# The searched run of a deep cross network kernel ends one tile further back, and the last tail phase too

## The chip, the cores and the metric

The kernel runs on one core of one Trainium2 chip. The metric is the device time in microseconds (us) of one execution. A core has a matrix engine (TensorE, PE in the profile), a vector engine (VectorE, DVE), a scalar engine (ScalarE, ACT), GpSimd (POOL) and a queue engine for DMA (SyncE, SP). They run side by side and wait for each other through semaphores. TensorE writes its results into PSUM, which has eight banks of 128 x 512 floats.

## The reference

```python
B, F, D, L = 16384, 26, 16, 6          # Din = F * D = 416
def reference(x0, ws, bs):             # x0 [B, 416], ws [6, 416, 416], bs [6, 416], all bf16
    x = x0
    for l in range(6):
        proj = jnp.einsum('bd,de->be', x, ws[l]) + bs[l]
        x = x0 * proj + x
    return x
```

Six layers follow one another. Each multiplies the running x by a 416 x 416 matrix, adds a bias, multiplies by the first input x0 element by element and adds x.

## The kernel before, in words

**Jobs, tiles, chunks.** The 16384 rows are cut into eight groups g of 2048 rows, and a job (g, l) is layer l of group g. In all but the last job the features lie on the partitions and the rows on the free axis. The 416 features are three blocks of 128 and a rest of 32. So a job has three tiles i = 0, 1, 2 of 128 output features, each cut into four chunks j of 512 rows, and a tail of 32 output features. The running x of a job lies in `xs` (three blocks) and `x3s` (the rest of 32, whose four chunks lie on the four quarters of the partitions).

**Two ways to compute a tile.** In the full way (`full`, line 659, and `rows32`, line 680) a tile is 12 matmuls that use all 128 rows of the array (three blocks by four chunks) and four matmuls 32 rows deep, one on each quarter of the array's rows, which run side by side. Tiles are paired so that the four-row parts of two neighbours stand together: mode "FR" does the full part first, "RF" the rows first, and "F1" is a single one that cuts its row part into pieces (line 674). In the searched run (`stream`, lines 1035 and 1039) every matmul is 32 rows deep. A chunk is then 13 matmuls, three for each of the four row groups and one more for the row group that holds its rest of 32. The four row groups work side by side on different chunks, and each row group adds into the chunk's bank in turn: within one chunk a row group waits until the one before it is through. `weave` searches for an order of these matmuls; four of them, one in each row group, take the place of one full matmul.

**Tails.** The 32 tail features of two or three jobs are computed together in a tail phase (`tails`, lines 694 and 706), one bank for each job, with four groups of 32 columns of the array side by side. A job (g, l + 1) needs the tail of (g, l).

**The order.** `items` is the list of all tiles and tail phases, and `where` says after which tile each tail phase stands. The searched run covers `items[s_lo:s_hi]`. What follows it is done in the full way: before the change these are the tiles (6,4)0, (6,4)1, (6,4)2, (7,4)0, (6,5)0, then the last tail phase with the tails of (7,4) and (6,5), then (6,5)1, (6,5)2, (7,4)1, (7,4)2. The last job, (7,5), comes after these in another form: rows on the partitions, four steps kk of four banks each (`nat_full`, line 1119, with ScalarE's copy on line 1171, VectorE's multiplication on line 1177 and addition on line 1183, and stores on line 1190).

**Evacuation.** ScalarE adds the bias and copies a bank to `tw` (line 574 in the searched run, 539 in the full way, 617 for tails). VectorE multiplies by x0 (lines 583, 548, 619) and adds x (lines 586, 553, 621). In the full way two neighbouring banks are read by one instruction, if their numbers follow one another.

**The output of group 6.** When the tail and the three tiles of (6,5) are done, `output(6)` puts on SP's queue, in this order: the transposing DMAs of feature block 0 and of block 1 from `xs` into `ost` (line 887), that of the tail into `ot3` (line 895), and two of half of block 2 (line 887). All DMAs of this end are issued by SP in program order, and each waits on SP for what it reads. The tail is copied from `ot3` into its place in `ost` by ScalarE (`spread("act")`, line 914). This copy stands in ScalarE's queue behind the evacuation of tile (7,4)1 and ahead of that of (7,4)2. `rest_turn(0)` and `rest_turn(1)` (line 935) transpose the results of (7,4)0 and (7,4)1 for the last job's additions, and two stores of group 6 (line 923) follow on SP's queue behind them.

Of the kernel before, what the change touches and what calls it, by code (L numbers as in the profile page):

```python
# [21 lines left out]
class Program:  # L22
# [12 lines left out]
    def add(self, eng, fn, reads=(), writes=(), lane=None, batch=None, hold=False, release=False, row=None):  # L35
        op = Op(eng, fn, lane, batch, row)
        deps = {}
        if eng == "pool":
            writes = list(writes) + ["pool"]
        for t in reads:  # L40
            w = self.writer.get(t)
            if w is not None:
                deps[id(w)] = (w, True)
        for t in writes:
            w = self.writer.get(t)
            if w is not None:
                deps[id(w)] = (w, True)
            for r in self.readers.get(t, ()):
                if id(r) not in deps:
                    deps[id(r)] = (r, False)  # L50
        for d, raw in deps.values():
            if d.lane is None and d.eng == eng and lane is None and (eng == "pe" or not raw):
                if row is None or d.row is None or row == d.row:
                    continue
            op.deps.append(d)
        for t in reads:
            self.readers.setdefault(t, []).append(op)
        for t in writes:
            self.writer[t] = op
            self.readers[t] = []  # L60
        if eng == "dve":
            if hold:
                self.flush()
                self.held = op
            else:
                self.queue[eng].append(op)
                if release:
                    self.flush()
        else:
            self.queue[eng].append(op)  # L70
        if lane is not None:
            batches = self.lanes.setdefault(lane, [])
            if not batches or batches[-1][0] != batch:
                batches.append((batch, []))
            batches[-1][1].append(op)
        return op
# [254 lines left out]
def bass_standalone__cross_network_dcn__recsys_kernel(  # L331
# [7 lines left out]
    L = ws.shape[0]  # L339
# [6 lines left out]
    LAST = NG - 1  # L346
# [9 lines left out]
    batches = []  # L356
# [582 lines left out]

    items = []  # L940
    where = {(b[0 if b in batches[4:-3] else min(1, len(b) - 1)], 0): b for b in batches[:-1]}
    where[((LAST - 1, L - 1), 0)] = batches[-1]
    del where[((0, 0), 0)]
    where[((0, 1), 0)] = where.pop(((1, 0), 0))
    tiles = [((1, 0), 0), ((1, 0), 1), ((0, 1), 0), ((0, 1), 1), ((0, 1), 2), ((1, 0), 2)]
# [11 lines left out]
    single = 0  # L957
    k = 0
    while k < len(items):
        if items[k][0] == "tails":  # L960
            if single % 2 == 0:
                nxt = k + 1
                if nxt < len(items) and items[nxt][0] == "tile":
                    items[k], items[nxt] = items[nxt], items[k]
                    single += 1
                    k += 1
            single = 0
        else:
            single += 1
        k += 1  # L970

    W_LOAD = {(1, 0): 3, (0, 2): 4, (1, 1): 5}
# [20 lines left out]
    mode = {}  # L993
    prev = None
    for n, it in enumerate(items):
        if it[0] == "tails":
            prev = None
        elif prev is None:
            mode[n] = "FR"
            prev = n  # L1000
        else:
            mode[n] = "RF"
            prev = None
# [61 lines left out]

    first_job()
    add("pool", lambda h: h.memset(brow[:, :], 0.0), writes=["brow"])
    s_lo, s_hi = items.index(("tile", (0, 2), 1)), items.index(("tile", (6, 4), 0))
    for n, it in enumerate(items):
        if n == s_lo:  # L1070
            stream(items[s_lo:s_hi])
# [196 lines left out]
```

## Time and profile before

| what | us |
|---|---|
| median of 3 runs | 472.18 (472.04 to 472.39) |
| the profiled execution: its time | 472.21 |
| the profiled execution: its span, first to last instruction | 470.4 |
| TensorE busy | 462.1 (98% of the span) |
| VectorE busy | 403.4 (86%) |
| ScalarE busy | 379.1 (81%) |
| the searched run ends, the full way begins | 424.18 |
| last tail phase (line 694, then 706) | 438.69 to 440.53 |
| tile (7,4)2 ends on TensorE | 452.18 |
| its last addition ends on VectorE | 456.92 |
| the last store is issued | 467.12 |

All places in the span are counted from its first instruction. A busy time is the sum over the instructions of an engine; instructions on one engine overlap a little, so that two additions of 0.69 us each may be shown as 1.28 us together. The chain that ended last is followed back from the last instruction, at each step to what released it. The profiled execution's 1.81 us outside the span are start and end that the trace does not show.

### The profile page before, as it was taken

How to read it: one execution, taken by the hardware profiler on the slowest of the kernel's cores; microseconds unless marked ns; L12 is line 12 of the kernel's file. 1: busy time of each engine (PE TensorE's matmuls, PEld its weight loads, DVE VectorE, ACT ScalarE, POOL GpSimd, SP SyncE). 2: the span in 40 equal slices, each digit the busy share in tenths (PEclk: the TensorE clock that was granted, in tenths of full speed). 3: DMA queues.
4: the chain of work that ended last, by engine and by line, in shares of the span. 5: the costliest groups of instructions: out<-in, count | busy, mean ns of one | idle time of the engine just before them, and what ended most of it. 6: DMA issues, size and time to landing. Idle time of an engine off the chain costs nothing.

```text
span 470.4 us, 17240 instructions
## 1 busy us (share of the span) xinstructions
PE 462.1 (98%) x7718; PEld 268.0 (57%) x7725; DVE 403.4 (86%) x700; ACT 379.1 (81%) x598; POOL 8.4 (2%) x15
## 2 busy tenths in 40 slices
PE   9999999999999999999999999999999999999995
PEld 5444476665655557566666567565455665653442
DVE  2897988888889888988989898988989888988887
ACT  4687788787878788787988878888788887877775
POOL 1000000000000000010001000000000000000000
PEclk9999999999999999999999999999999999999999
DMA  8985849101002967094667993880000194139689
GB/s 225 185 175 141 159 113 186 30 3 26 2 5 34 184 189 143 19 146 148 134 105 114 227 146 81 169 248 3 25 2 3 29 167 124 34 59 216 127 148 293
DMA packets 139086, 53.75 MB, mean 114 GB/s; under 512 B 112762, under 2 KB 138500, under 8 KB 139012
## 3 DMA queue, kind: packets, MB, share of 16 engines
q1 hardware_dynamic: 138856, 52.54, 53.1%
q8 instruction: 60, 0.98, 0.9%
q10 hardware_dynamic: 156, 0.11, 0.1%
q14 instruction: 14, 0.11, 0.1%
HBM read 5.97 MB, written 13.63 MB: 42 GB/s over the span
## 4 chain that ended last, share of the span: by engine, by line
PE 92%; DVE 5%; ACT 1%; DMA 1%; issue 0%; DVEq 0%; SPq 0%; ACTq 0%
PE ps L1035 67%; PE ps L659 7%; PE ps L1039 6%; PE ps L706 6%; PE ps L647 2%; PE ps L694 1%; DVE x L1183 1%; PE ps L680 1%; DVE x L1177 1%; PE ps L778 1%; ACT tw L539 1%; DVE x L553 1%; DVE tw L548 1%; DMA ot<-x 1%; DVE x L586 1%; DVE tw L583 1%
## 5 line engine op out<-in xcount | busy, mean ns | idle before, releaser
L1035 PE MATMUL ps<-x,wm 32*128 32x512 bf16 x5856 | 349.9, 375 | 0.6 <-DVE ts L613 0.6
L574 ACT ACTIVATE tw<-ps,bias 128x512 bf16<-128x512 f32 x488 | 305.1, 687 | 42.0 <-PE ps L1035 26.9
L1035 PEld LDWEIGHTS ps<-x,wm 32*128 32x128 bf16 x5856 | 213.5, 92 | 123.4 <-issue 3.2
L583 DVE TENSOR_TENSOR tw<-tw,x 128x1024 bf16<-128x1024 bf16 x244 | 166.0, 690 | 41.2 <-ACT tw L574 40.5
L586 DVE TENSOR_TENSOR x<-tw,x 128x1024 bf16<-128x1024 bf16 x244 | 158.3, 686 | 0.4
L1039 PE MATMUL ps<-x,w 32*128 32x512 bf16 x488 | 147.6, 374 | 0.0
L539 ACT ACTIVATE tw<-ps,bias 128x1024 bf16<-128x1024 f32 (+1 forms) x48 | 40.7, 917 | 14.9 <-PE ps L680 11.7
L1039 PEld LDWEIGHTS ps<-x,w 32*128 32x128 bf16 x488 | 42.0, 92 | 5.8
L659 PE MATMUL ps<-x,wm 128*128 128x512 bf16 x181 | 41.3, 380 | 1.0 <-issue 1.0
L617 ACT ACTIVATE ts<-ps,bias 128x512 bf16<-128x512 f32 x33 | 21.0, 685 | 20.4 <-PE ps L694 20.4
L706 PE MATMUL ps<-x,wm 128*32 128x512 bf16 x564 | 33.6, 380 | 0.0
L659 PEld LDWEIGHTS ps<-x,wm 128*128 128x128 bf16 x188 | 17.3, 98 | 23.8 <-issue 3.8
L548 DVE TENSOR_TENSOR tw<-tw,x 128x1024 bf16<-128x1024 bf16 (+1 forms) x41 | 25.5, 634 | 5.2 <-ACT tw L539 4.9
L553 DVE TENSOR_TENSOR x<-tw,x 128x1024 bf16<-128x1024 bf16 (+1 forms) x41 | 24.4, 631 | 0.0
L706 PEld LDWEIGHTS ps<-x,wm 128*32 128x32 bf16 x564 | 13.5, 96 | 17.8 <-ACT tw L574 3.4
L621 DVE TENSOR_TENSOR x<-ts,x 128x512 bf16<-128x512 bf16 x47 | 18.3, 418 | 0.0
L613 DVE SCALAR_TENSOR_TENSOR ts<-ps,bias,x 128x512 bf16<-128x512 f32 x14 | 10.5, 749 | 6.1 <-PE ps L694 5.9
L916 POOL COPY ost<-ot 128x512 bf16<-128x512 bf16 x6 | 7.0, 1158 | 413.4 <-DMA ot<-x 413.4
L619 DVE TENSOR_TENSOR ts<-ts,x 128x512 bf16<-128x512 bf16 x33 | 13.6, 418 | 0.0
L1119 PE MATMUL ps<-wm,x 128*128 128x416 bf16 x48 | 9.8, 340 | 0.7 <-DVE x L553 0.7
L1171 ACT ACTIVATE x<-ps 128x416 bf16<-128x416 f32 x16 | 7.7, 517 | 2.1 <-PE ps L1119 1.9
L806 DVE COPY x<-ps 128x512 bf16<-128x512 bf16 x5 | 2.0, 423 | 8.4 <-PE ps L796 8.3
(50 smaller groups left out, 78.2 us busy)
## 6 DMA issues: line engine op xcount, KB each, us to landing
out_dram<-ost SPq DMA_DIRECT2D x6, 1664.0 KB, 8.2
x<-x SPq DMA_DIRECT2D x24, 96.0 KB, 2.2
x<-in_x_dram SPq DMA_DIRECT2D x8, 208.0 KB, 4.3
x<-in_x_dram SPq DMA_DIRECT2D x4, 416.0 KB, 6.8
out_dram<-ost SPq DMA_DIRECT2D x2, 832.0 KB, 5.6
wm<-in_ws_dram SPq DMA_DIRECT2D x5, 312.0 KB, 3.5
x<-x SPq DMA_DIRECT2D x22, 64.0 KB, 2.2
out_dram<-x SPq DMA_DIRECT2D x3, 416.0 KB, 4.8
```

The lines of the kernel that those rows point to most:

```text
L539: add("act", lambda h, a=a, w=w, b0=b0: h.activation(tw[r][:, a * CH:(a + w) * CH], psum[:, b0 * CH:(b0 + w) * CH], ACT_F.Identity, bias=b ...
L548: add("dve", lambda h, a=a, e=e: h.tensor_tensor(tw[r][:, a * CH:e * CH], tw[r][:, a * CH:e * CH], x0s[s0][:, i * GC + a * CH:i * GC + e * ...
L553: add("dve", lambda h, a=a, e=e: h.tensor_tensor(xs[so][:, i * GC + a * CH:i * GC + e * CH], tw[r][:, a * CH:e * CH], src(i, a, e), ALU.ad ...
L574: add("act", lambda h: h.activation(tw[r][:, j * CH:(j + 1) * CH], bank(b), ACT_F.Identity, bias=bias[:, i, l:l + 1], scale=1.0), reads=[( ...
L583: add("dve", lambda h: h.tensor_tensor(tw[r][:, o], tw[r][:, o], x0s[s0][:, c], ALU.mult), reads=[("tw", r, k) for k in both] + [x0_tok(s0 ...
L586: add("dve", lambda h: h.tensor_tensor(xs[so][:, c], tw[r][:, o], src(i, a, a + 2), ALU.add), reads=[("tw", r, k) for k in both] + [stok(i ...
L617: add("act", lambda h: h.activation(ts[r][:, :], bank(b), ACT_F.Identity, bias=bias[:, 3, l:l + 1], scale=1.0), reads=[("ps", b), "bias"], ...
L621: add("dve", lambda h: h.tensor_tensor(x3s[so][:, :], ts[r][:, :], res, ALU.add), reads=[("ts", r)] + rtok, writes=[("x3", so), ("x3", so, ...
L659: add("pe", lambda h, t=t, j=j, k=k, w=w: h.matmul(bank(banks[j])[:, k * w:(k + 1) * w], wm[l][:, t, ecols], src(t, j, j + 1)[:, k * w:(k ...
L706: add("pe", lambda h, t=t, j=j, src=src, l=l, b=b, ro=ro, qo=qo: h.matmul(psum[qo, b * CH:(b + 1) * CH], wm[l][:, t, NT * P:D], src(t, j, ...
L1035: add("pe", lambda h, l=l, t=t, j=j, b=b, q=q, ecols=ecols, src=src, kw=kw: h.matmul(bank(b), wm[l][q, t, ecols], src(t, j, j + 1)[q, :], ...
L1039: add("pe", lambda h, l=l, b=b, q=q, ecols=ecols, s3=s3, kw=kw: h.matmul(bank(b), w3[l][q, ecols], s3[q, :], **kw), reads=tok3 + [("w3", l ...
```

## The change

The last tail phase is attached to tile (6,5)1 in place of (6,5)0, so that three tiles follow it in place of four. The searched run ends before tile (6,4)1 in place of (6,4)0. The pairing of the tiles, which decides their modes, begins anew at (6,4)1, and so does the count `single` that decides whether a tail phase is moved by one tile.

```diff
     items = []
     where = {(b[0 if b in batches[4:-3] else min(1, len(b) - 1)], 0): b for b in batches[:-1]}
-    where[((LAST - 1, L - 1), 0)] = batches[-1]
+    where[((LAST - 1, L - 1), 1)] = batches[-1]
+    behind = ("tile", (LAST - 1, L - 2), 1)
...
         else:
-            single += 1
+            single = 1 if items[k] == behind else single + 1
         k += 1
...
     for n, it in enumerate(items):
+        if it == behind:
+            prev = None
         if it[0] == "tails":
             prev = None
...
-    s_lo, s_hi = items.index(("tile", (0, 2), 1)), items.index(("tile", (6, 4), 0))
+    s_lo, s_hi = items.index(("tile", (0, 2), 1)), items.index(behind)
```

The end of the list of items, with the modes, before:

```
searched run ... (7,3)1 (7,3)2 |
(6,4)0 FR, (6,4)1 RF, (6,4)2 FR, (7,4)0 RF, (6,5)0 F1, tails (7,4)+(6,5),
(6,5)1 FR, (6,5)2 RF, (7,4)1 FR, (7,4)2 RF
```

and after:

```
searched run ... (7,3)1 (7,3)2 (6,4)0 |
(6,4)1 FR, (6,4)2 RF, (7,4)0 FR, (6,5)0 RF, (6,5)1 F1, tails (7,4)+(6,5),
(6,5)2 FR, (7,4)1 RF, (7,4)2 RF
```

The line numbers of the kernel after are three higher from `stream` on.

## The prediction

> **What bounds the kernel now.** I read first the page's busy times and then the chain that ended last, because the change touches only the end of the order.
>
> ```profile
> PE 462.1 (98%) x7718; PEld 268.0 (57%) x7725; DVE 403.4 (86%) x700; ACT 379.1 (81%) x598; POOL 8.4 (2%) x15
> ```
>
> TensorE is busy in 98% of the span, and nothing in the change takes matmuls away. So any gain has to come from the stretch in which TensorE no longer sets the end. The chain, in order of time, says where that begins:
>
> ```profile
> 440.53 2.59 PE ps L647 x48
> 443.12 0.37 PE ps L680 x4
> 443.48 2.27 ACT tw L539 x3
> ...
> 448.87 0.61 DVE x L553
> 449.49 0.16 SPq L887
> 449.64 0.05 issue
> 449.69 2.96 DMA ot<-x
> 452.65 0.02 issue
> 452.67 0.63 ACT ost L914
> 453.30 1.16 ACT tw L539 x2
> ...
> 456.25 0.67 DVE x L553 x2
> 456.92 1.20 DVE x L1139 x2
> 458.12 0.49 DVE x L1177
> 458.61 0.44 issue
> ```
>
> TensorE leaves the chain at 443.48. From there it runs over the additions of the tiles behind the tail phase, SP, the transposition of group 6's tail (ot<-x) and ScalarE's copy of it (L914), behind which the evacuation of (7,4)2 is queued. From 454 to 466.8 it is VectorE. The timeline shows what VectorE (first four rows) and ScalarE (next four) waited for:
>
> ```profile
> 450.66 0.69 DVE L548 TENSOR_TENSOR tw<-tw,x 128x1024 bf16<-128x1024 bf16 x1 [0.58 <-ACT tw L539]
> 451.66 0.69 DVE L548 TENSOR_TENSOR tw<-tw,x 128x1024 bf16<-128x1024 bf16 x1 [0.32 <-ACT tw L539]
> 453.91 0.42 DVE L548 TENSOR_TENSOR tw<-tw,x 128x512 bf16<-128x512 bf16 x1 [0.35 <-ACT tw L539]
> 454.49 0.43 DVE L548 TENSOR_TENSOR tw<-tw,x 128x512 bf16<-128x512 bf16 x1 [0.15 <-ACT tw L539]
> ...
> 445.96 2.12 ACT L539 ACTIVATE tw<-ps,bias 128x1024 bf16<-128x1024 f32 x2 [0.22 <-PE ps L659]
> 449.36 2.27 ACT L539 ACTIVATE tw<-ps,bias 128x512 bf16<-128x512 f32 x3 [1.28 <-PE ps L680]
> 452.67 0.63 ACT L914 ACTIVATE ost<-ot 128x512 bf16<-128x512 bf16 x1 [1.04 <-DMA ot<-x]
> 453.21 2.40 ACT L539 ACTIVATE tw<-ps,bias 128x512 bf16<-128x512 f32 x4
> ```
>
> VectorE stands idle for 0.58 + 0.32 + 0.35 + 0.15 = 1.40 us between 450.07 and 456.92, and ScalarE for 1.04 us on the tail's transposition. Last I read the DMAs of the last 13.4 us (40 slices from 457.0 to 470.4):
>
> ```profile
> DMA  0999999999999999999999999999999999930000
> ```
>
> The DMA engines are full from 457.4 to 468.7, so the stores could set the end as well.
>
> **The change part by part.** The order of the instructions is the same in both kernels up to the middle of the stretch ahead of the searched run's last tail phase.
>
> *(6,4)0 goes into the searched run.* The full way gives 24 matmuls in 5.13 us, 0.214 us each; a tile is 12 of these and one slot of rows, 13 slots or 2.78 us, and so are four chunks in the searched run (52 matmuls, four to a slot). What follows on TensorE up to the tile in 32-column pieces (L647) is the same sequence of full tiles, rows and tail phase, one tile's name further on, with as many switches between the forms. So that tile ends later by 2.78 us plus what the run's end loses more than before. Before, 90 matmuls follow the run's last tail phase: 22.5 slots, 4.82 us; they take 418.15 to 424.18, 6.03 us, so 1.21 are lost, to row groups that wait for another one in the same bank and to the run-out, where some row groups have finished. After, 138 matmuls follow it, and 4 more stand ahead of it. The new list ends with four matmuls all on row group 3, behind chunks that the other three have finished; the old one ends with two on one row group. Following both lists row group by row group at 0.214 us, with a short pause wherever a chunk passes to another row group, gives 5.84 us for the old one (6.03 measured) and 8.87 for the new one. With one slot for the 4 matmuls ahead that is 3.24 us more, against 2.78: **0.46 us lost**. Bounds: nothing (a run-out as good as before), and 1.21 (the loss of this stretch once more). I take 0.46, as the same counting came within 0.2 us of the measured row.
>
> *Three tiles behind the tail phase.* The piece tile ends at 443.12 + 3.24 = 446.36; it is now (6,5)2. By the distances before, ScalarE begins its evacuation 0.35 us later, at 446.71, and needs 2.12 (two pairs of banks; the instruction list shows whole pairs for all these tiles, against 2.27 with a split pair before): 448.83. VectorE must be free by then: its tail work, which ended at 444.33, moves by 3.24 to 447.57, ahead of the first pair at 447.8. Then a multiplication of 0.69 and two additions, 1.28 together and overlapping by 0.08, end at 450.74. (7,4)1 is "RF" now, so its evacuation waits for no rows behind it: its full part begins 0.70 us behind the piece tile, at 447.06, and ends 2.57 later at 449.63; ScalarE starts 0.42 ahead of that (as at 445.96 before, where the tile in the middle ended at 446.38) and ends at 451.33. VectorE does (7,4)1 in 2.48 us without a wait, up to 453.22.
>
> *The tail's transposition.* On SP, block 1 of group 6 waited for VectorE until 447.66, was issued at 447.69 and held SP for 1.95 us; the tail followed at 449.69. Now block 1 is (6,5)1, ahead of the tail phase, and its last addition moves from (6,5)0's 442.99 by 3.24 to 446.23. SP issues it until 448.2, and the tail, ready at 447.57, is issued then and lands 2.96 later, at 451.2: as ScalarE comes free at 451.33. The wait of 1.04 goes. The copy (0.54 us up to the next start) ends at 451.87, and (7,4)2's four evacuations at 454.3; TensorE has its last chunk by 452.8. VectorE, which comes to them at 453.2, now finds them ready: eight operations at 0.347 (the seven from 454.49 to 456.92) end at 456.0. **0.92 us earlier** than 456.92; the 1.40 us of idle time go, and 0.46 of lost run-out and small shifts come off.
>
> *Behind it.* SP's later issues follow: the halves of block 2 (2.64 us for both) from 450.15, the transpositions of (7,4)1 from 452.8 (454.15 before), the stores of group 6 from 456.0 (457.36), 1.36 earlier. The 0.44 us "issue" at 458.61 stands ahead of the additions that read the transposed (7,4)1; this wait shrinks by up to 0.43, of which at most 0.2 reaches the end, since ScalarE's last copy ends at 465.97 and VectorE takes it up at about 466.2. The last store (104 KB) lands 2.8 us after its issue; small copies on the chip land after 2.2 in the median (64 and 96 KB), so up to 0.6 of it is waiting behind full DMA engines, which start 1.36 earlier. From these the end moves by 0.92 at least and 0.92 + 0.6 at most; I take 1.3, near the DMAs' 1.36, since they are full to the end. All other work moved (evacuation of (6,4)0 by single chunks, 4 x 0.69 on ScalarE in place of 2.12) lies beside TensorE: ScalarE and VectorE both stood idle between 420 and 427 (VectorE for 1.84 us, ScalarE for 1.08), and both wait for TensorE again before the tail phase.
>
> The sum: the profiled execution's 472.21 (span 470.4 and 1.81 around it; 0.03 above the median, so no correction) less 1.3 is **470.9**.
>
> **The rivals.**
>
> *The run's end costs more.* In the new list 13 chunks follow the last tail phase, and ScalarE needs 0.6 to 0.69 us for each plus 1.26 for the tails. The first full tile takes its fourth bank from the last chunk but one, which ScalarE, counted from the chunks' ends at these prices, leaves at 427.9 to 428.2; TensorE wants it at 428.2. With the upper price and the row groups' bound of 1.21, TensorE is 0.9 us later than in my sum, and the end at 471.8, within 0.2% of before. For it: the margin is nil. Against: before, a bank was taken the same way at no visible cost.
> The Trainium skill's page "TensorEngine Tiling (Array Packing)", section Performance Considerations, says that tiling the array speeds up TensorE but not the evacuation of PSUM, which can then become the bottleneck. It speaks against a longer searched run; the trace so far has ScalarE at 81% with TensorE at 98%, so it bears it out at the run's end at most, and by it the time would be that 471.8.
>
> *Slower: the tail's transposition comes late.* It now starts only 0.6 us after the tail is ready, with SP's queue ahead of it and the copy L914 ahead of the whole last evacuation. Other transpositions of this line (895) landed after 2.5 to 4.4 us, and the transpositions of line 887 after up to 6.4. At 4.4 it lands at 452.65, as before, and the gain is gone up to the DMAs' share; each us more goes into the end. From 5.4 on it is slower by more than 0.2%: at 6.4 ScalarE is 2.0 us later than before, 474.2. Against it: the one of before landed after 2.96, behind the same transposition.
>
> *The end is bound elsewhere.* If the last job's steps are paced by TensorE's matmuls on line 1119 and by the last stores, VectorE's gain stays in front of them: half of 0.92, 471.7.
>
> **How the numbers follow.** 0.2% is 0.94 us, about what a measurement of this kernel can tell from no change. Forecast (faster by 1.3, at least 0.94) 0.53. Run's end 0.17 and bound elsewhere 0.10, both within 0.2%. Slower 0.20: the late tail 0.11, and 0.09 for a run's end worse than its bound. The forecast's own range is 470.2 (no loss at the run's end) to 471.3. The range to 473.3 takes in "no change" and the lesser of the slower cases.
>
> **What would show it.** Right: full-array matmuls begin near 427.4; L914 without a wait; VectorE without idle time between 449 and 456; the last evacuation's addition ends near 456.0; the first group 6 store near 456.0. Wrong: full-array matmuls after 428.2, or a wait of ScalarE for "ot" again.

## The result, and the profile after

The changed kernel takes 471.08 us in the median of 11 runs (470.73 to 471.68), the kernel before 472.45 in the median of 11 (472.04 to 472.81). The ratio is 0.9973, with a 95% interval of 0.9963 to 0.9982: 1.4 us faster by the medians and 1.3 by the ratio, at the forecast of 1.3. The two profiled executions stand at 472.21 and 471.08 us, with spans of 470.4 and 469.3; so 1.1 us are to be found in the traces.

The busy times of the page after (its first part) hardly differ:

```profile
PE 463.3 (99%) x7761; PEld 268.9 (57%) x7761; DVE 403.8 (86%) x700; ACT 378.8 (81%) x596; POOL 7.3 (2%) x15
```

Next the chain that ended last in the changed kernel, in order of time: start, length, what.

```profile
427.51 2.70 PE ps L659 x12
...
443.86 2.59 PE ps L647 x48
446.45 0.38 PE ps L680 x4
446.83 2.11 ACT tw L539 x2
448.94 0.02 issue
448.96 0.54 DVE tw L548
449.50 2.52 DMA ot<-x
452.02 0.02 issue
452.05 0.63 ACT ost L914
452.68 1.16 ACT tw L539 x2
...
454.91 3.28 DMA x<-x
458.20 0.03 issue
458.23 0.02 DVEq L168
458.25 0.19 issue
458.43 1.09 DVE x L1186 x2
...
465.89 0.29 DVE x L1186
466.18 0.28 DVEq L175
```

The tail's transposition (ot<-x) is still in the chain, and was issued only 0.19 us earlier than before (449.69). The chain puts a multiplication of VectorE ahead of it (448.96), but this link is inferred from semaphores: the multiplication was not over at 449.50, and SP's rows below show that the issue of block 1 ended at 449.45 and the tail's followed. What changed are the waits around it, as the timeline rows of VectorE, ScalarE and SP show:

```profile
449.57 1.29 DVE L553 TENSOR_TENSOR x<-tw,x 128x1024 bf16<-128x1024 bf16 x2
450.77 1.42 DVE L548 TENSOR_TENSOR tw<-tw,x 128x1024 bf16<-128x1024 bf16 x2
452.11 1.29 DVE L553 TENSOR_TENSOR x<-tw,x 128x1024 bf16<-128x1024 bf16 x2
453.31 0.97 DVE L548 TENSOR_TENSOR tw<-tw,x 128x512 bf16<-128x512 bf16 x2
...
449.35 2.12 ACT L539 ACTIVATE tw<-ps,bias 128x1024 bf16<-128x1024 f32 x2 [0.42 <-PE ps L659]
452.05 0.63 ACT L914 ACTIVATE ost<-ot 128x512 bf16<-128x512 bf16 x1 [0.58 <-DMA ot<-x]
...
442.95 6.50 SPq L887 DMA_TRANSPOSE ost<-x  x2
449.50 1.26 SPq L895 DMA_TRANSPOSE ot<-x  x1
...
456.43 1.14 SPq L923 DMA_DIRECT2D out_dram<-ost  x2
```

These rows of VectorE carry no wait in brackets any more: it goes from (6,5)2 to (7,4)1 and on to (7,4)2 with gaps of 0.2 us at most, where it stood idle for 1.40 us before. The "DMA x<-x" of the chain is the transposition of (7,4)1, which now lands just as VectorE comes to the additions that read it. ScalarE still waits for the tail's transposition, for 0.58 us in place of 1.04. The last addition of (7,4)2 ends at 456.30 (456.92 before), and the last addition of the chain on VectorE at 466.18 (466.80): 0.62 us. (One more addition, outside the chain, ends 0.28 us later in both.) Group 6's first store is issued at 456.43 (457.36). The rest of the gain lies behind VectorE. The DMA view gives kilobytes and microseconds from issue to landing of the last two stores:

```profile
out_dram<-x SPq DMA_DIRECT2D x1, 104.0 KB, 2.3
out_dram<-x ACTq DMA_DIRECT2D x1, 104.0 KB, 2.3
```

They took 2.8 before: 0.5 us. 0.62 and 0.5 make the 1.1 us of the two spans. This is bookkeeping at the last store, which was issued earlier and waited less; it does not say that two causes add up. The table of the experiments shows that the end of this kernel follows another event: the landing of the second half of (7,4)1's transposition on SP's queue, behind which the DMA engines carry group 6's stores and all that follows. It landed at 459.29 before and at 458.20 after, 1.1 us earlier.

### The profile page after: what moved, and what is told of

The parts are those of the page before. It is cut to its first block, busy times and chain, and to the rows that moved or that the text cites. A ratio compares the mean times of both kernels' runs of the same rounds, so it can differ in the third digit from the quotient of the medians.

```text
span 469.3 us, 17315 instructions
## 1 busy us (share of the span) xinstructions
PE 463.3 (99%) x7761; PEld 268.9 (57%) x7761; DVE 403.8 (86%) x700; ACT 378.8 (81%) x596; POOL 7.3 (2%) x15
## 4 chain that ended last, share of the span: by engine, by line
PE 93%; DVE 3%; ACT 1%; DMA 1%; issue 0%; DVEq 0%; ACTq 0%
PE ps L1038 68%; PE ps L659 7%; PE ps L1042 6%; PE ps L706 6%; PE ps L647 2%; PE ps L694 1%; DVE x L1186 1%; PE ps L680 1%; PE ps L778 1%; PE ps L796 1%; DVE x L1180 1%; DMA x<-x 1%; ACT tw L539 1%; DVE x L586 1%; DVE tw L583 1%; ACT tw L574 1%
## 5 line engine op out<-in xcount | busy, mean ns | idle before, releaser
L1042 PE MATMUL ps<-x,w 32*128 32x512 bf16 x492 | 149.3, 374 | 0.0
L539 ACT ACTIVATE tw<-ps,bias 128x1024 bf16<-128x1024 f32 (+1 forms) x42 | 37.9, 970 | 15.2 <-PE ps L680 11.6
L548 DVE TENSOR_TENSOR tw<-tw,x 128x1024 bf16<-128x1024 bf16 (+1 forms) x39 | 24.3, 633 | 6.2 <-ACT tw L539 5.9
L659 PEld LDWEIGHTS ps<-x,wm 128*128 128x128 bf16 x176 | 16.2, 98 | 21.9 <-issue 3.6
L553 DVE TENSOR_TENSOR x<-tw,x 128x1024 bf16<-128x1024 bf16 (+1 forms) x39 | 23.1, 629 | 0.0
L613 DVE SCALAR_TENSOR_TENSOR ts<-ps,bias,x 128x512 bf16<-128x512 f32 x14 | 10.5, 749 | 6.3 <-PE ps L694 6.1
```

Of the source, the lines that this page charges most:

```text
L539: add("act", lambda h, a=a, w=w, b0=b0: h.activation(tw[r][:, a * CH:(a + w) * CH], psum[:, b0 * CH:(b0 + w) * CH], ACT_F.Identity, bias=b ...
L548: add("dve", lambda h, a=a, e=e: h.tensor_tensor(tw[r][:, a * CH:e * CH], tw[r][:, a * CH:e * CH], x0s[s0][:, i * GC + a * CH:i * GC + e * ...
L553: add("dve", lambda h, a=a, e=e: h.tensor_tensor(xs[so][:, i * GC + a * CH:i * GC + e * CH], tw[r][:, a * CH:e * CH], src(i, a, e), ALU.ad ...
L659: add("pe", lambda h, t=t, j=j, k=k, w=w: h.matmul(bank(banks[j])[:, k * w:(k + 1) * w], wm[l][:, t, ecols], src(t, j, j + 1)[:, k * w:(k ...
L1042: add("pe", lambda h, l=l, b=b, q=q, ecols=ecols, s3=s3, kw=kw: h.matmul(bank(b), w3[l][q, ecols], s3[q, :], **kw), reads=tok3 + [("w3", l ...
```

## The experiments

Theory A is the prediction's: the place of the tail phase makes the gain, through VectorE, which no longer waits for ScalarE. Its rivals: B, the run's end and the whole pairs of banks; C, ScalarE's wait for the tail's transposition alone; D, formed from the first runs: the end is set as much by when the DMA engines get to group 6's stores. T is when the second half of (7,4)1's transposition lands, and the column before the last has how long the last store took to land and where that was. Times are against the kernel before, in runs on the same chip.

| kernel | ratio (95% interval) | VectorE's chain ends | first group 6 store issued | T | last store: took, lands at | span |
|---|---|---|---|---|---|---|
| before | 1 | 466.80 | 457.36 | 459.29 | 2.8, 469.90 | 470.4 |
| changed (the result's profile) | 0.9973 (0.9963 to 0.9982) | 466.18 | 456.43 | 458.20 | 2.3, 468.80 | 469.3 |
| changed, once more | 0.9975 (0.9965 to 0.9984) | 466.37 | 456.40 | 458.19 | 2.1, 468.79 | 469.3 |
| longer run alone | 0.9997 (0.9989 to 1.0006) | 466.92 | 457.18 | 458.96 | 2.3, 469.53 | 470.0 |
| later tail phase alone | 0.9972 (0.9961 to 0.9982) | 465.65 | 455.46 | 458.16 | 2.8, 468.76 | 469.2 |
| before, tail first on SP | 0.9985 (0.9976 to 0.9994) | 466.41 | 455.99 | 458.87 | 2.7, 469.46 | 469.9 |
| changed, tail first on SP | 0.9988 (0.9980 to 0.9997) | 466.29 | 457.15 | 459.04 | 3.0, 469.58 | 470.1 |
| two tiles behind | 1.0018 (1.0008 to 1.0027) | 467.12 | 457.37 | 459.13 | 3.4, 470.87 | 471.4 |
| before, quarter stores | 0.9975 (0.9965 to 0.9986) | 466.77 | 457.63 | 459.51 | 1.7, 468.82 | 469.3 |
| changed, quarter stores | 0.9962 (0.9948 to 0.9976) | 466.32 | 456.46 | 458.17 | 1.7, 468.38 | 468.9 |
| before, stores on GpSimd | 1.0041 (1.0024 to 1.0059) | 472.35 | 455.83 | 465.10 | 1.7, 474.40 | 474.9 |
| changed, stores on GpSimd | 1.0059 (1.0046 to 1.0072) | 471.09 | 454.74 | 463.83 | 1.7, 473.15 | 473.6 |
| later tail phase, stores on GpSimd | 1.0047 (1.0030 to 1.0065) | 471.01 | 453.93 | 463.76 | 1.7, 473.07 | 473.6 |

Two columns settle between A and D how the end is reached. In the seven rows above "two tiles behind", with whole stores on SP, the last store lands 10.5 to 10.6 us after T, while it lands 2.4 to 3.3 us after VectorE's end, with no order in it; the two profiles of the changed kernel have VectorE's ends 0.19 us apart and land within 0.01. In the five kernels with small stores, or with the stores moved to GpSimd, it lands 2.05 or 2.06 us after VectorE's end. So the last store can be read as held by two bounds, of which the later counts: VectorE's end and 2.05 us, and, with whole stores on SP, T and 10.6 us. For the kernel before these are 468.85 and 469.89, for the changed one 468.23 and 468.80. In both the second is the later: the gain that is seen is that of T, and VectorE's 0.62 us would not have been paid without it.

**Both parts.** The changed kernel once more, as the measure for the runs beside it.

> The changed kernel as it is, beside the kernel before on the same chip as the three that follow, so that they can be set against it. By the first comparison 1.2 to 1.4 us faster. Its VectorE should end the last addition of (7,4)2 near 456.3 (456.92 before) and the last store should land after about 2.3 us (2.8 before).

Measured: 471.18 us against 472.31, ratio 0.9975 (0.9965 to 0.9984), span 469.3. The distance repeats, though 1.1 is a little less than was expected. The evacuation of (7,4)2 ends at 456.38, near the 456.3 expected, and the last store lands after 2.1 us, not 2.3.

**The longer run alone.**

```diff
# against the changed kernel
-    where[((LAST - 1, L - 1), 1)] = batches[-1]
+    where[((LAST - 1, L - 1), 0)] = batches[-1]
...
-            single = 1 if items[k] == behind else single + 1
+            single += 1
```

> Only the searched run ends one tile further back; the tail phase stays behind (6,5)0 with four tiles behind it, as before. Theory A (the gain comes from the place of the tail phase: block 1's transposition and the tail's are no longer in the way, and (7,4)1 is evacuated without waiting for rows): this part alone costs what the run's end loses, 0.55 us by the changed kernel's trace, so 0.3 to 0.6 slower, with ScalarE's wait for the tail's transposition about 1 us as before. Rival B (the gain comes from the run's end and the whole pairs of banks): at least 0.8 faster.

Measured: 472.11 us, 0.03% under the kernel before, with no change inside the interval. ScalarE waits 1.02 us for the tail's transposition, as theory A has it, and the evacuation of (7,4)2 ends on VectorE 0.12 us later than before. The 0.3 to 0.6 us that this part was to cost do not show. Rival B, which asked for at least 0.8, falls: this part gives nothing that can be measured in the medians. In the profile, 0.3 us under the median, T comes 0.33 us earlier than before, although the transposition is issued 0.12 later; the next run shows why.

**The later tail phase alone.**

```diff
# against the kernel before
-    where[((LAST - 1, L - 1), 0)] = batches[-1]
+    where[((LAST - 1, L - 1), 1)] = batches[-1]
...
-            if single % 2 == 0:
+            if single % 2 == 0 and items[k][1] is not batches[-1]:
```

The second edit keeps the tail phase from being moved one tile further.

> Only the tail phase moves: the searched run ends before (6,4)0 as in the kernel before, and the tail phase stands behind (6,5)1 with three tiles behind it, as in the changed kernel. TensorE changes form twice more than before, since (6,5)1 has no rows behind it. Theory A: all of the gain is here, and the run's 0.55 us is not paid, less about 0.2 to 0.3 for the two changes of form: 1.4 to 1.7 faster than before, a little faster than the changed kernel. Rival B: within 0.4 of the kernel before.

Measured: 471.04 us, as fast as the whole change. All of the gain is here. But VectorE ends at 465.65, 0.53 ahead of the changed kernel, and this lead is not in the time. The timeline of ScalarE and SP:

```profile
450.93 0.64 ACT L914 ACTIVATE ost<-ot 128x512 bf16<-128x512 bf16 x1
...
448.01 1.61 SPq L895 DMA_TRANSPOSE ot<-x  x1
449.92 2.61 SPq L887 DMA_TRANSPOSE ost<-x  x2
452.58 2.71 SPq L935 DMA_TRANSPOSE x<-x  x2
455.46 1.90 SPq L923 DMA_DIRECT2D out_dram<-ost  x2
```

ScalarE no longer waits for the tail's transposition at all, and the stores are issued 1 us ahead of the changed kernel's; yet the last store lands after 2.8 us, not 2.3. The issue was earlier, the transfer was not. That took theory A's measure, VectorE's end, off the table as the only one, and led to theory D.

The traces show what held the transfer. The last two numbers of these rows are the DMA engines' share and GB/s in the microsecond from 456 to 457, for the kernel before, the changed one and this one:

```profile
456.00:457.00 1.00, 1.00 (x11) 0.56 (x12) 1.00 (x4) 0.57 (x3) 0.00 (x0) 1.00 1.00 20
456.00:457.00 1.00, 1.00 (x12) 0.56 (x10) 1.00 (x3) 0.94 (x3) 0.00 (x0) 1.00 0.97 191
456.00:457.00 1.00, 1.00 (x16) 0.31 (x13) 0.99 (x3) 1.00 (x4) 0.00 (x0) 1.00 0.39 10
```

And this is the DMA view from 452 to 457.5: one line of packets of the kind "instruction", with packets and MB, and the two halves of (7,4)1's transposition, with the median us to landing. The kernel before has the first two lines, the changed one the third alone:

```profile
q8 instruction: 1, 0.02, 1.0%
x<-x SPq DMA_TRANSPOSE x2, 4.1
...
x<-x SPq DMA_TRANSPOSE x2, 3.4
```

In the kernel before and in this one, one instruction packet falls into the transposition, at 455.66 and 455.21, and within half a microsecond the packets of the transposition stand still for about 1.5 us, as the packet records of the traces have it. In the changed kernel the last such packet comes at 446.9. The same line divides all the kernels with the stores on SP: the four with the packet there (the two named, "before, tail first" and "before, quarter stores") have halves that land after 3.8 to 4.9 us, the six without it after 3.2 to 3.4. All four have the shorter searched run, all six the longer run or a later end of it. That the packet is the cause is argued from this coincidence; no run moved it alone.

So of the 1.1 us of the change, 0.63 are SP's, which issues the second half at 454.91 and not at 455.54, and 0.47 are the landing after 3.28 us and not 3.75, which goes with the packet's place. In this kernel the second half is issued at 453.96, 1.58 us earlier than before, but takes 4.20 us.

**The tail first on SP.** In both kernels, with the same edit:

```diff
         turn(0)
-        if g == LAST - 1:
-            turn(1)
         add("sp", lambda h: h.dma_start_transpose(ot3[:, :, :], x3s[s3][:, :]),
...
         else:
+            turn(1)
             turn(2, 0, 2)
```

> The kernel before with one thing else: on SP the tail's transposition of group 6 (ot) stands ahead of block 1's. The tail is ready at 444.33, so it is issued near 445.1 and lands near 448, and ScalarE no longer waits 1.04 us for it. This tells apart which idle time made the gain. If the wait for the tail's transposition made it (rival C), this alone gives all of it, 1.1 to 1.4 faster. Theory A with both causes: VectorE's idle 0.35 + 0.15 us goes, its 0.58 + 0.32 ahead of (7,4)1 stays, and ScalarE's copy moves away: 0.5 to 0.8 us at VectorE, and with the stores moved by as much as SP is freed, 0.6 to 1.0 faster in all.

Measured: 471.58 us, 0.7 us faster. ScalarE goes to the copy of the tail (line 913 in this kernel) without a wait. VectorE still waits ahead of (7,4)1 and ends 0.39 earlier; 0.1 us more comes off at the last store's landing, and T comes 0.42 earlier. So C explains a part of the gain and not the whole: a little over half of it by the medians.

> The changed kernel with the tail's transposition (ot) ahead of block 1's on SP. It removes what is left of ScalarE's wait there, 0.58 us. Theory A: VectorE was busy with (7,4)1 for most of that wait, so at most 0.2 us comes off at VectorE: 1.2 to 1.6 faster than the kernel before. If ScalarE's wait still set the end in the changed kernel (rival C), 0.6 more than the changed kernel, 1.8 to 2.0 faster.

Measured: 471.78 us, slower than the changed kernel in place of faster, by 0.6 us when each is set against its own kernel before. The 1.2 to 1.6 us of theory A are missed as well: it is 0.6 us faster than the kernel before. VectorE's evacuation of (7,4)2 ends at 456.17, 0.13 ahead of the changed kernel's, so C falls there; but SP now reaches the stores later, as its timeline shows:

```profile
454.25 2.72 SPq L934 DMA_TRANSPOSE x<-x  x2
457.15 1.14 SPq L922 DMA_DIRECT2D out_dram<-ost  x2
```

and the last two stores in the DMA view, with KB and microseconds to landing:

```profile
out_dram<-x SPq DMA_DIRECT2D x1, 104.0 KB, 2.9
out_dram<-x ACTq DMA_DIRECT2D x1, 104.0 KB, 3.0
```

The stores are issued 0.72 us later than in the changed kernel, and the last one lands after 3.0 us in place of 2.3, while VectorE ends within 0.11 us of the changed kernel's. The 0.8 us between the two profiles lie in the queue: the second half of (7,4)1's transposition is issued 0.73 us later, since block 1, ready near 446.4, now stands behind the tail, which SP issues at 447.79; T is 459.04 in place of 458.20.

**Two tiles behind.** The change taken one tile further.

```diff
# against the changed kernel
-    where[((LAST - 1, L - 1), 1)] = batches[-1]
-    behind = ("tile", (LAST - 1, L - 2), 1)
+    where[((LAST - 1, L - 1), 2)] = batches[-1]
+    behind = ("tile", (LAST - 1, L - 2), 2)
```

> The same change taken one tile further: the searched run ends before (6,4)2 and the tail phase stands behind (6,5)2, with two tiles behind it. Block 2 and the tail of group 6 are then ready only behind the tail phase, about 2.8 us later than in the changed kernel, with ScalarE's copy of the tail still ahead of the last evacuation. The slower rival of the prediction (a late tail's transposition holds ScalarE) must show here: ScalarE waits 2 to 4 us for ot, and the end comes 0.5 to 3 us later than in the kernel before. If the place of the tail phase does not matter, it is as fast as the changed kernel.

Measured: 473.20 us, 0.85 us slower than before. The sign is the expected one, but the wait is smaller:

```profile
452.99 0.63 ACT L914 ACTIVATE ost<-ot 128x512 bf16<-128x512 bf16 x1 [1.26 <-DMA ot<-x]
```

1.26 us, not 2 to 4. The tail is ready at 450.37, 2.7 us later than in the changed kernel, but there SP held it back until 449.50; here it is issued at once, at 450.45, so it comes only 0.95 us later. VectorE ends 0.32 later than before, but T comes 0.17 earlier, and T and 10.6 us would make an end 0.2 us ahead of the kernel before. The loss arises behind T: the second of group 6's large stores lands after 7.9 us, where it took 6.5 to 6.7 in the others with whole stores on SP, and everything behind it is as late. In this kernel alone an instruction packet falls among the stores, at 462.53. That it holds them up is likely and only argued. So the sign came out for another reason than the expected one: this run does not show that a late tail's transposition costs time.

**Quarter stores.** In both kernels the two last stores of group 6 write one of four row blocks, 0.42 MB in place of 1.66; three quarters of group 6's rows are not written.

```diff
-        add("sp", lambda h: h.dma_start(rows.rearrange(pat, j=j1 - j0, k=KK), o),
+        kn = 1 if g == LAST - 1 else KK
+        add("sp", lambda h: h.dma_start(rows.rearrange(pat, j=j1 - j0, k=KK)[:, :, 0:kn, :], o[:, :, 0:kn, :]),
```

> The kernel before, but the two last stores of group 6 write only the first of four row blocks (0.42 MB in place of 1.66 MB; three quarters of group 6's rows are not written). If the DMA engines, full from 457.4 on, hold up the last store, it now lands after 2.2 to 2.3 us in place of 2.8, with VectorE's end unmoved at 466.8: 0.4 to 0.6 faster. If the 2.8 us are the store's own, no difference.

Measured: 471.18 us, 1.2 us faster, twice what was expected, with VectorE's end at 466.77. The same two rows of the DMA view:

```profile
out_dram<-x SPq DMA_DIRECT2D x1, 104.0 KB, 1.7
out_dram<-x ACTq DMA_DIRECT2D x1, 104.0 KB, 1.7
```

So a last store with little ahead of it lands after 1.7 us, and 1.1 us of the 2.8 are waiting. With VectorE's end unmoved, relief of the DMA engines alone brings as much as the change did.

> The changed kernel with the same quarter stores (three quarters of group 6's rows are not written). Its last store already landed after 2.3 us, so if the waiting behind full DMA engines is what came off, there is nothing left to gain: within 0.2 of the changed kernel, 1.1 to 1.5 faster than the full kernel before, and 0.6 to 0.9 (VectorE's part) faster than the kernel before with quarter stores. If not, the landing stays at 2.3 and the distance between the two quarter kernels stays 1.1 to 1.4.

Measured: 470.70 us, 0.4 us under the changed kernel; landing again after 1.7 us. There was 0.6 us of waiting left, so the first expectation misses, and 1.7 us under the kernel before is more than the 1.1 to 1.5 expected. The distance between the two quarter kernels is 0.5 us in the medians, a little under the 0.6 to 0.9 expected; the last store lands 0.44 us earlier, and VectorE ends 0.45 earlier. With small stores VectorE's gain is paid.

**Group 6's stores on GpSimd.** In three kernels GpSimd issues the two stores of group 6, so that they no longer stand in SP's queue. The edit also gives them semaphores of their own and takes them out of the order of GpSimd's other work; the calls alone are shown.

```diff
...
-    store(LAST - 1, 0, 2)
-    store(LAST - 1, 2, NJ)
+    store(LAST - 1, 0, 2, "pool")
+    store(LAST - 1, 2, NJ, "pool")
```

> The kernel before, but the two last stores of group 6 are issued by GpSimd, which stands idle there, in place of SP, where they queue behind the transpositions of (7,4)1. Theory D (the end is set by when the DMA engines begin with group 6's 1.66 MB, not by VectorE): the stores can start when block 2's halves have landed, 1 to 2 us earlier, VectorE's end stays within 0.3 of 466.8, and the kernel is 0.5 to 1.2 faster. Theory A (VectorE's end carries the gain): no more than 0.3 faster. If the earlier stores slow the transpositions of (7,4)1, VectorE's additions wait longer than the 0.44 + 0.21 us of before, and part of it is lost.

> The changed kernel with the same two stores on GpSimd. Theory D: the stores start up to 1.5 us earlier than at 456.43, the last store then lands after less than 2.3 us (1.7 with no queue, from the quarter stores), and it is 0.3 to 0.6 faster than the changed kernel, 1.6 to 1.9 faster than before. Theory A: as the changed kernel.

> Only the tail phase moved (as in the run of the later tail phase alone, whose VectorE ended 0.5 us ahead of the changed kernel's, but whose last store waited 1.1 us behind full DMA engines), with the two stores on GpSimd. Theory D: the stores no longer queue behind the transpositions of (7,4)1, the last store lands after about 2 us, and this beats both kernels: 1.8 to 2.3 faster than before. If the DMA engines are held by the transpositions themselves and not by the order on SP's queue, it stays at the 1.3 of the run without GpSimd.

Measured: 473.53, 475.26 and 474.74 us, all slower than before, with a spread of 2 to 4 us within each kernel. The profile of the first is its slowest execution, at 476.71, so its rows show more of the loss than the median has; the other two stand near their medians. The condition that was set down as a risk decides. The timeline of VectorE in the kernel before with these stores:

```profile
458.45 1.10 DVE L1177 TENSOR_TENSOR x<-x,x 128x832 bf16<-128x832 bf16 x2
459.47 0.58 DVE L1183 TENSOR_TENSOR x<-x,x 128x832 bf16<-128x832 bf16 x1
465.19 0.59 DVE L1183 TENSOR_TENSOR x<-x,x 128x832 bf16<-128x832 bf16 x1 [5.13 <-DMA x<-x]
```

A store that is issued 1.5 us earlier, from a queue of its own, runs beside the transpositions of (7,4)1. In all three kernels it comes 0.1 us ahead of the issue of their second half, which lands after 9.2 us (9.0 and 9.7 in the other two) in place of at most 4.4, and VectorE's second addition waits 5.13 us for it. The last store, with little left ahead of it, lands after 1.7. So the order on SP's queue, transpositions first and stores behind them, protects the last job; starting the stores earlier in this way is not to be had for nothing. Whether it is the time or GpSimd's queue that does the harm, these runs do not separate. None of the kernels was clearly faster than the changed one.

## Why the prediction was right, point by point

*The run's end.* Right. The full-array matmuls begin at 427.51; 424.18 + 2.78 + 0.46 gave 427.42. The loss is 0.55 us. (The row from which the prediction takes 24 matmuls in 5.13 us counts 23. Nothing hangs on it: the changed kernel's rows, 12 in 2.70 and 24 in 5.29, give 0.216 for each further one, against 0.214.) The rival of a worse run's end did not come: ScalarE freed the banks in time, and no wait for a bank shows ahead of 427.51 in the chain.

*Three tiles behind the tail phase.* Right, row by row: the piece tile ends at 446.45 (446.36 forecast), ScalarE starts (6,5)2 at 446.81 (446.71), VectorE's additions of it end at 450.86 (450.74), those of (7,4)1 at 453.40 (453.22), with no wait between. VectorE's 0.58 and 0.32 us of idle time ahead of (7,4)1 went.

*The tail's transposition.* Wrong in one term, the 1.95 us for which block 1's issue was to hold SP. Block 1 was issued at 446.35, close to the forecast (446.25), but held SP for 3.10 us, so the tail was issued at 449.50 and not at 448.2. It landed after 2.52 us, and ScalarE waited 0.58 us where none was forecast. The evacuation of (7,4)2 ended at 456.30 and not at 456.0: VectorE gained 0.62 and not 0.92. The slower rival, a late tail, was thus there in a small measure at ScalarE; no run shows that it cost time at the end.

*Behind it.* The stores came 0.93 us earlier and not 1.36: SP issued block 1 1.34 us earlier than before, lost 1.15 in its longer issue and won 0.43 back, since the tail's issue held it for 1.26 us and not 1.68; the other 0.3 us came with the shorter issue of (7,4)1's second half, 1.34 in place of 1.65. The 0.44 and 0.21 us "issue" of the chain were read as waits of VectorE for the transposed (7,4)1. They are links of the chain and no idle time: VectorE's rows there (458.04 for 1.10 us, 459.05 for 1.09) leave no gap. VectorE's end moved by no more than its evacuation did, and the 0.2 us allowed for this wait did not reach the end. The waiting of the last store was mis-sized: the prediction took 2.2 us for a landing with no queue, from copies of other sizes, and so 0.6 us of waiting; it is 1.7, and 1.1 of waiting. Of this the change took 0.5.

*The sum.* 0.62 + 0.5 in place of 0.92 + 0.38: the two terms err in opposite directions, and the total came out at 1.4 by the medians and 1.1 by the profiles, with 1.3 forecast. The nearness of the number is in part luck. The prediction chose 1.3 because the DMA engines, full to the end, would start 1.36 us earlier. That is the bound that held, but the start came 0.93 us earlier, and of the 1.10 by which T moved 0.47 go with an instruction packet that the prediction did not know of. Its other bound, VectorE's 0.92 us "at least", is not one: while T and 10.6 us come later, VectorE's gain adds nothing. The rival "bound elsewhere" was thus right on the place, the last stores, and wrong in holding them still. In the kernel with the later tail phase alone, half a microsecond of VectorE's further gain stays in front of the stores.

*The place of the gain.* The prediction had named the longer run as a cost of 0.46 and the tail phase's place as the gain. The tail phase alone gives 0.28% and the longer run alone nothing measurable. The longer run is thus not needed for the gain; with it VectorE ends 0.53 us later than with the tail phase alone, about the 0.55 lost at the run's end. That the two are equal in time goes with T, 458.20 and 458.16: with the tail phase alone SP issues the second half of (7,4)1's transposition 0.95 us earlier, and it takes 0.91 longer, with the instruction packet beside it. So theory A is shown for the place of the gain, by the run that moved the tail phase alone. The way it gave, through VectorE, is not shown: the end follows SP's queue and the transfers.

## What to carry to other kernels

At the end of a kernel that is bound by one engine, the chain leaves that engine, and what counts is the last producer and the transfer queue together: note for each version when the last producer ends, when the large stores were issued, and how long the last small store takes to land. Here a store that landed in 2.8 us, where one with little ahead takes 1.7, told that the DMA engines were a second clock, and the later of the two clocks alone sets the end. Set the landings of several versions side by side: the event from which the end keeps the same distance in all of them, here T and 10.6 us, is the one to move. Before a transfer is moved ahead in a queue, look for what it will then run beside: here earlier stores cost the transpositions more than the stores gained.

## What the runs showed of the hardware that was not expected

The issue of a transposing DMA of one block (line 887) held SP for 1.95 to 2.03 us when it came 3.2 to 4.7 us behind the one before it on SP (blocks 0 and 1 in the kernel before), and for 3.10 us when it came 2.5 and 3.4 us behind (the same blocks in the changed kernel). That the earlier one was still under way is the likely cause. The issues of blocks 0 and 1 in all the runs, 26 of them, fall in two groups by it: where the DMA before had 1.95 us or less to go to its landing, SP was held for 1.79 to 2.27 us (14 issues), and where it had 2.44 us or more to go, for 2.78 to 3.47 (12 issues). No run changed this alone.

The two transpositions of (7,4)1, which landed after 3.3 to 4.4 us in the kernels before and after, took up to 9.2, 9.0 and 9.7 us with 1.66 MB of stores beside them from GpSimd's queue.

A packet of the kind "instruction", 16 KB, went with a pause of about 1.5 us in a transposition that was under way: in the kernel before the DMA engines moved 20 GB/s from 456 to 457, in the changed one, without the packet, 191. Not every such packet goes with a pause: in the second profile of the changed kernel the one at 447.0, with a transposition under way, shows none. Where the last one comes depends on the kernel: at 455.2 to 456.0 in the six with the shorter searched run, at 446.8 to 447.1 in the changed one and those with the same searched run, and at 462.5 in the one with two tiles behind.
